# Attention masks moved from TensorE to VectorE in two chunks, and one score product a head instead of two in seven

## The chip, the cores and the metric

One Trainium2 chip, one of its cores. The metric is the device time of one execution in microseconds; the kernel before takes 721.85 us (median of three runs, 721.52 to 722.61).

## The reference

Three parts follow each other: windowed attention, a dense layer pair with an ELU between, and a layer of eight experts in which a token belongs to one expert by a greedy assignment with a capacity. Only the attention is touched here:

```python
# q, k, v: (4, 8, 576, 64), float32; window = 64, scale = 1/8
scores = scale * np.matmul(q, k.transpose(0, 1, 3, 2))
rel = pos[:, None] - pos[None, :]
mask = (rel >= 0) & (rel < window)          # a query sees itself and the 63 before it
scores = np.where(mask, scores, -1000000000.0)
scores = scores - np.max(scores, axis=-1, keepdims=True)
attn = np.exp(scores)
attn = attn / (np.sum(attn, axis=-1, keepdims=True) + 1e-09)
out = np.matmul(attn, v)
# x: (2304, 512) = out, heads side by side; h = x @ w_in; g = elu(h); y = g @ w_out
# logits = y @ w_gate; assignment of 2304 tokens to 8 experts of 288; relu(y @ w1[e]) @ w2[e]
```

## The kernel before

The 2304 tokens are 18 chunks of 128 (c = 0 to 17). A sequence has 576 tokens, four and a half chunks, so a sequence begins at chunk 0, in the middle of chunk 4, at chunk 9 and in the middle of chunk 13. A chunk is two blocks of 64 queries. A block of queries needs 128 keys: its own 64 and the 64 ahead of them. For block 1 both halves lie in the chunk; for block 0 the half ahead is the second half of the chunk before.

A chunk goes through steps that are written as functions:

- `att_s1` transposes queries and keys on TensorE (four 128x128 transposes each, into the PSUM tiles "tp") and copies them to SBUF on ScalarE as `QT` and `KT`. `KT[c]` holds the keys as [rows of two heads, half of the chunk, pair of heads, 64 keys].
- `att_s2` makes the scores: the PSUM tiles `SC[0]` and `SC[1]`, one for a block, [128, 4, 128]. On the partitions stand the 64 queries of one of two heads, along them four pairs of heads and 128 keys. With `on_pe` true a mask product (line 301) writes the mask into the whole tile first, 0 or -2^40, from an identity and a bf16 mask tile, and the score products add to it. With `on_pe` false the score products write alone. Each product has 64 rows and 64 columns of weights (the queries of one head in one block). Block 1 takes one product a head over 128 keys (line 312, both halves of the chunk). Block 0 takes two: the own 64 keys (line 316) and, unless a sequence begins there, the 64 ahead from `KT[c - 1]` (line 319). The operands are float32, and each product is two passes, thus two rows in the trace. Eight heads in two blocks are 16 products of 64 columns on line 316 and 319 together and 8 of 128 on line 312: 48 passes.
- `att_exp` takes the row maxima on VectorE (line 336) and the exponentials on ScalarE (line 338). Where the mask isn't in the scores yet, VectorE adds it first, from PSUM to the SBUF tile `P` (line 333), and maximum and exponential read `P`. Now that is so from chunk 10 on.
- `att_norm` divides by the sums on VectorE (line 351); `att_s3` transposes `P` on TensorE (line 359) and copies it on ScalarE (line 361); `att_s4` multiplies it with the values (line 369) and hands the rows to the first layer (lines 386, 387). Block 1's values are the chunk's own, `V[c]`; block 0's are a tile `VP[c]` with the own 64 in its first half of partitions and the 64 ahead in the second, filled by two DMAs from SP.

In `attention` the order of one round is: `att_s1(c)`, the two `att_s3(c - 1)`, `att_s2(c)`, `att_exp(c)`, `att_norm(c)`, `att_s4(c - 1)`. From chunk 4 on the rounds are woven with the dense layers: `weave` takes from several streams in proportion to given weights, and so writes the program's order. Around this change the order is: the first layer of tile 2 with chunk 7; the second layer of tile 0 with chunks 8 to 10 and the rest of the preparation of w_out (`prep_wout`: three bit operations, a ScalarE and a VectorE step for each of 16 pieces, the last of which stands behind `att_s3(8, 1)`); the second layer of tile 1 with the next three rounds; that of tile 2 with three more, with the gate's weights (`prep_g2`) and some logits; the first layer of tile 3 with what is left of attention. A scheduler then orders each engine's instructions with a clock of its own: an instruction that is not ready by that clock lets later ones of the program pass. Each engine runs its queue in order, so an instruction whose operands are late holds up those behind it.

The PSUM banks are "mm" (three, the layers' products), "tp" (two, transposes and small products), "sc" (two, the scores) and "pv" (one). `a2` is a pool of SBUF tiles that is opened before the second layer of tile 1, when the rounds have reached chunk 10.

Of the kernel before, what the change touches and what calls it, by code (L numbers as in the profile page):

```python
# [7 lines left out]
F32 = mybir.dt.float32  # L8
# [37 lines left out]
def attention_moe_moe2_kernel(ctx: ExitStack, tc: tile.TileContext, q, k, v, w_in, w_out, w_gate, w1, w2, out):  # L46
    nc = tc.nc
# [11 lines left out]
    ND = DM // 128  # L59
# [17 lines left out]
    def bank(tag, bufs, shape=(128, 512), dt=F32):  # L77
        return ps.tile(list(shape), dt, name="ps_" + tag, tag=tag, bufs=bufs)
# [30 lines left out]
    masks = consts.tile([128, 2, 2, 128], BF)  # L109
# [125 lines left out]
            last["rows"] = ins.ins  # L235


    QN, KN, QT, KT, V, VP, P, PT, XT = ({} for _ in range(9))

    def rows(src, n, m):  # L240
        b, s = divmod(n, S)
        return src[b, :, s:s + m, :].rearrange("h s d -> s h d")

    def load(src, c, name, bufs=3):
        t = att.tile([128, H, D], F32, name=name, bufs=bufs)
        n = 128 * c
        while n < 128 * (c + 1):
            m = min(128 * (c + 1) - n, S - n % S)
            p0 = n - 128 * c
            nc.sync.dma_start(t[p0:p0 + m], rows(src, n, m))  # L250
            n += m
        return t
# [6 lines left out]
    def load_v(c):  # L259
        if c < NCH:  # L260
            V[c] = load(v, c, "vn")
            if c:
                VP[c] = att.tile([128, H, D], F32, name="vp", bufs=3)
                nc.sync.dma_start(VP[c][:64], rows(v, 128 * c, 64))
                nc.sync.dma_start(VP[c][64:], rows(v, 128 * c - 64, 64))

    def att_s1(c):
        KT[c] = att.tile([128, 2, ND, 64], F32, name="kt", bufs=3)
        pq = bank("tp", 2, [128, ND, 128])
        for i in range(ND):  # L270
            with tc.issue_after(last["qt", c]) if c in (2, 3, 4) else ExitStack():
                nc.tensor.transpose(pq[:, i], QN[c][:, 2 * i:2 * i + 2, :].rearrange("p h d -> p (h d)"), ident)  # L272
        QT[c] = att.tile([128, ND, 128], F32, name="qt", bufs=2)
        if c == 1:
            nc.vector.tensor_scalar(QT[c], pq, 0.125, None, op0=OP.mult)
        else:
            nc.scalar.activation(QT[c], pq, AF.Copy, scale=0.125)
        pk = bank("tp", 2, [128, 2, ND, 64])
        for i in range(ND):
            t = nc.tensor.transpose(pk[:, :, i], KN[c][:, 2 * i:2 * i + 2, :].rearrange("p h d -> p (h d)"), ident)  # L280
        if c == 0:
            last["kt"] = t.ins
        if c == 1:
            nc.vector.tensor_copy(KT[c], pk)
        else:
            nc.scalar.activation(KT[c], pk, AF.Copy)

    SC = {}

    def att_s2(c):
        for blk in range(2):
            SC[blk] = bank(*(("mm", 3) if c == 1 else ("sc", 2)), [128, ND, 128])
        half = [slice(0, 64), slice(64, 128)]
        first = [int((128 * c + 64 * blk) % S == 0) for blk in range(2)]
        on_pe = c < 10 or bool(first[0])
        for blk in range(2 if on_pe else 0):
            with tc.issue_after(last["kt"]) if c < 2 and c + blk else ExitStack():  # L300
                nc.tensor.matmul(SC[blk], identb, masks[:, blk, first[blk], None, :].to_broadcast([128, ND, 128]),
                                 start=True, stop=False)
        for i in range(ND):
            for n in range(2):
                for blk in range(2):
                    for h in range(2):
                        if blk == 1 and n == 1:
                            continue
                        r, o = half[h], half[h ^ blk]
                        w = QT[c][r, i, 64 * blk:64 * blk + 64]  # L310
                        if blk == 1:
                            t = nc.tensor.matmul(SC[1][o, i], w, KT[c][r, :, i], start=not on_pe, stop=not on_pe or i == ND - 1)  # L312
                            if c < 3:
                                last["sc"] = last["qt", c + 1] = t.ins
                        elif n == 0:
                            nc.tensor.matmul(SC[0][o, i, :64], w, KT[c][r, 0, i], start=not on_pe,  # L316
                                             stop=not on_pe or i == ND - 1 and bool(first[0]))
                        elif not first[0]:
                            nc.tensor.matmul(SC[0][o, i, 64:], w, KT[c - 1][r, 1, i], start=not on_pe,
                                             stop=not on_pe or i == ND - 1)  # L320

# [2 lines left out]
    def att_exp(c):  # L324
        mx = att.tile([128, 2, ND], F32, name="mx")
        rs = RS[c] = att.tile([128, 2, ND], F32, name="rs")
        for blk in range(2):
            first = [int((128 * c + 64 * b) % S == 0) for b in range(2)]
            P[c, blk] = att.tile([128, ND, 128], F32, name="sm", bufs=4)
            sc = SC[blk]  # L330
            if c >= 10 and not first[0]:
                sc = P[c, blk]
                nc.vector.tensor_tensor(sc, SC[blk], masks[:, blk, first[blk], None, :].to_broadcast([128, ND, 128]),
                                        op=OP.add)
            with tc.issue_after(last["max"]) if c == 1 and blk else ExitStack():
                last["max"] = nc.vector.tensor_reduce(mx[:, blk], sc, axis=AX.X, op=OP.max, negate=True).ins  # L336
            for i in range(ND):
                nc.scalar.activation(P[c, blk][:, i], sc[:, i], AF.Exp, bias=mx[:, blk, i:i + 1],
                                     accum_out=rs[:, blk, i:i + 1])
# [55 lines left out]
    def attention(a, b):  # L395
        for c in range(a, b + 1):
            if c < b:
                att_s1(c)
                load_qk(c + 3)
                yield 1500  # L400
            if c > a:
                att_s3(c - 1, 0)
                yield 500
                att_s3(c - 1, 1)
                yield 500
            if c < b:
                att_s2(c)
                att_exp(c)
                att_norm(c)
            if c > a:  # L410
                att_s4(c - 1)
                load_v(c + 2)
            yield 1500

    def early():
        def scores(c):
            att_s2(c)
            att_exp(c)
            att_norm(c)

        for part in (lambda: att_s1(2), lambda: load_qk(5), lambda: scores(2), lambda: att_s1(3), lambda: load_qk(6),
                     lambda: scores(3), lambda: att_s3(2, 0), lambda: att_s3(2, 1), lambda: att_s4(2), lambda: load_v(5),
                     lambda: att_s3(3, 0), lambda: att_s3(3, 1), lambda: att_s4(3), lambda: load_v(6)):
            with tc.high_priority():
                part()
            yield 1

    a2 = []
    a2_ctx = ExitStack()

    NF32 = 1
# [636 lines left out]
    for c in range(2):  # L1068
        att_s1(c)
        load_qk(c + 3)  # L1070
    for c in range(2):
        att_s2(c)
        att_exp(c)
# [114 lines left out]
```

## Time and profile before

| | |
|---|---|
| median of three runs | 721.85 us (721.52 to 722.61) |
| profiled execution | 725.0 us, its span 723.3 us |
| granted TensorE clock, mean | 0.998 |
| TensorE busy | 702.1 us, 97% |
| VectorE busy | 434.9 us, 60% |
| ScalarE busy | 354.7 us, 49% |
| GpSimd busy | 166.7 us, 23% |
| chain that ended last | TensorE 72%, issue 14%, VectorE 6%, ScalarE 4% |

Busy shares are means over stages; products are pipelined and their records overlap, so what one costs in a run of equal ones is the distance from start to start. In the rows PE is TensorE's products, PEld its weight loads, DVE VectorE, ACT ScalarE, POOL GpSimd; L312 is line 312. A time is in microseconds from the start of the span.

### The profile page before, as it was taken

What the parts mean: (1) busy time and instruction counts of PE and PEld (TensorE: products, weight loads), DVE (VectorE), ACT (ScalarE), POOL (GpSimd) and SP (SyncE); (2) the same over time, 40 slices, a digit from 0 to 9 for tenths busy, and PEclk for the clock granted to TensorE, in tenths of its full rate; (3) what the DMA queues carried; (4) which work ended last, traced back from release to release, by engine and by line L of the source; (5) the groups of instructions that cost most, each with busy time, mean ns of one, the idle gap of its engine ahead of it and who ended that gap; (6) DMA issues with size and microseconds to landing.
All of it is one profiled execution on the core that took longest, in us unless ns stands there. A gap on an engine that the chain in (4) does not pass through costs nothing.

```text
span 723.3 us, 15666 instructions
## 1 busy us (share of the span) xinstructions
PE 702.1 (97%) x6350; PEld 431.5 (60%) x6350; DVE 434.9 (60%) x1027; ACT 354.7 (49%) x853; POOL 166.7 (23%) x267
## 2 busy tenths in 40 slices
PE   7889999999999999999999999999989999999996
PEld 4768778656655555554545544444766566566662
DVE  4888998964343766455544556665556556465630
ACT  4369988776454646444454231010155554564630
POOL 2000000020100354444441343544232210210001
PEclk9999999999999999999999999999999999999999
DMA  9997564597466721001010220220179787677401
GB/s 232 365 246 153 137 149 132 143 169 160 105 123 128 110 51 61 1 1 59 1 58 18 74 86 18 88 74 30 59 193 337 236 262 253 237 232 232 144 30 44
DMA packets 137881, 94.56 MB, mean 131 GB/s; under 512 B 116496, under 2 KB 116752, under 8 KB 137808
## 3 DMA queue, kind: packets, MB, share of 16 engines
q1 hardware_dynamic: 134848, 83.85, 43.3%
q0 software_dynamic: 2960, 9.70, 4.1%
q8 instruction: 50, 0.82, 0.5%
q14 instruction: 23, 0.19, 0.1%
HBM read 73.94 MB, written 9.70 MB: 116 GB/s over the span
## 4 chain that ended last, share of the span: by engine, by line
PE 72%; issue 14%; DVE 6%; ACT 4%; POOL 2%; DMA 1%; SPq 0%; POOLq 0%; ACTq 0%; DVEq 0%
PE ps_mm L555 25%; PE ps_mm L477 20%; PE ps_mm L1022 6%; PE ps_pv L369 3%; PE ps_tp L1006 2%; PE ps_sc L1006 2%; PE ps_mm L461 2%; PE ps_tp L359 2%; POOL out_dram L990 1%; PE ps_sc L749 1%; DVE mx L336 1%; PE ps_sc L312 1%; PE ps_sc L316 1%; PE ps_tp L272 1%; PE ps_tp L280 1%
## 5 line engine op out<-in xcount | busy, mean ns | idle before, releaser
L555 PE MATMUL ps_mm<-slab,g 128*128 128x512 f16 (+1 forms) x912 | 202.1, 367 | 0.0
L477 PE MATMUL ps_mm<-xt,slab 128*128 128x512 f16 (+1 forms) x960 | 174.6, 336 | 1.5 <-DVE xt L387 0.8
L477 PEld LDWEIGHTS <-slab 128*128 128x128 f16 x960 | 91.2, 98 | 69.0 <-issue 2.5
L555 PEld LDWEIGHTS <-g 128*128 128x128 f16 x912 | 79.8, 98 | 69.6
L1022 PE MATMUL ps_mm<-xet,slab 128*128 128x288 f16 (+2 forms) x768 | 98.1, 280 | 2.7 <-issue 2.2
L923 DVE SCALAR_TENSOR_TENSOR slab<-raw,slab 128x512 f16<-128x512 f32 x112 | 73.6, 687 | 39.0 <-ACT slab L922 33.7
L1022 PEld LDWEIGHTS <-slab 128*128 128x128 f16 x840 | 76.9, 98 | 28.9 <-issue 5.9
L480 ACT ACTIVATE r<-ps_mm 128x512 f32<-128x512 f32 x64 | 38.3, 599 | 65.7 <-PE ps_mm L477 52.0
L1006 PEld LDWEIGHTS <-h 128*32 128x32 f16 (+2 forms) x768 | 43.6, 99 | 44.7 <-issue 4.2
L922 ACT ACTIVATE slab<-raw 128x512 f16<-128x512 f32 x112 | 65.6, 624 | 0.3 <-DMA raw<-in_moe_w_dram 0.3
L489 DVE TENSOR_TENSOR r<-ps_mm,r 128x512 f32<-128x512 f32 x64 | 44.0, 688 | 29.7 <-POOL r L488 28.1
L591 ACT ACTIVATE r<-ps_mm 128x512 f32<-128x512 f32 x17 | 10.1, 595 | 100.8 <-PE ps_mm L555 90.0
L494 DVE TENSOR_TENSOR g<-r,g 128x512 f16<-128x512 f32 x64 | 44.3, 693 | 24.3 <-POOL g L493 22.9
L1006 PE MATMUL ps_sc<-slab,h 128*32 128x512 f16 (+2 forms) x384 | 53.2, 380 | 0.6 <-issue 0.3
L1006 PE MATMUL ps_tp<-slab,h 128*32 128x512 f16 (+2 forms) x384 | 52.6, 379 | 0.0
L1029 DVE SCALAR_TENSOR_TENSOR h<-ps_mm,h 128x288 f16<-128x288 f32 x61 | 27.7, 455 | 35.6 <-ACT h L1028 35.4
L1028 ACT ACTIVATE h<-ps_mm 128x288 f16<-128x288 f32 x61 | 25.0, 410 | 42.0 <-PE ps_mm L1022 41.4
L488 POOL TENSOR_SCALAR r<-r 128x512 f32<-128x512 f32 x48 | 33.6, 699 | 48.5 <-ACT r L481 48.2
L481 ACT ACTIVATE r<-r 128x512 f32<-128x512 f32 x64 | 40.5, 633 | 1.5
L990 POOL DMA_INDIRECT out_dram<-orow,idx x18 | 17.6, 979 | 93.5 <-ACT orow L1012 91.2
L493 POOL TENSOR_SCALAR g<-r 128x512 f16<-128x512 f32 x48 | 30.1, 627 | 38.4 <-DVE r L489 33.8
L537 POOL TENSOR_TENSOR xs<-r,xs 128x512 f16<-128x512 f32 x17 | 20.0, 1178 | 81.6 <-ACT xs L592 50.1
(235 smaller groups left out, 1016.4 us busy)
## 6 DMA issues: line engine op xcount, KB each, us to landing
raw<-in_moe_w_dram SPq DMA_DIRECT2D x32, 1024.0 KB, 5.4
slab<-in_moe_w_in_dram SPq DMA_DIRECT2D x16, 512.0 KB, 8.1
st<-in_moe_w_out_dram SPq DMA_DIRECT2D x16, 512.0 KB, 6.3
x2d<-xs SPq DMA_DIRECT2D x18, 256.0 KB, 2.8
vp<-in_v_dram SPq DMA_DIRECT2D x34, 128.0 KB, 4.4
qn<-in_q_dram SPq DMA_DIRECT2D x16, 256.0 KB, 5.1
kn<-in_k_dram SPq DMA_DIRECT2D x16, 256.0 KB, 4.9
vn<-in_v_dram SPq DMA_DIRECT2D x16, 256.0 KB, 4.9
```

The lines of the kernel that those rows point to most:

```text
L477: nc.tensor.matmul(ph[:, i], wi[d, (f + i) // 8][:, a, (f + i) % 8 * 128:((f + i) % 8 + 1) * 128], XT[t][:, b, d, :n], start=m == 0, stop= ...
L480: nc.scalar.activation(r, ph, AF.Relu, scale=-1.0 / A_H)
L481: last["act"] = nc.scalar.activation(r, r, AF.Exp, scale=-1.0).ins
L488: nc.gpsimd.tensor_scalar(r, r, -1.0, A_H, op0=OP.add, op1=OP.mult)
L489: nc.vector.tensor_tensor(r, ph, r, op=OP.max)
L493: last["pool"] = nc.gpsimd.tensor_scalar(hi, r, 1.0, 1.0, op0=OP.mult, op1=OP.mult).ins
L494: nc.vector.tensor_tensor(lo, r, hi, op=OP.subtract)
L555: pe(nc.tensor.matmul(px, g[:, f % fg, a, 128 * i:128 * i + 128], wo[f // 2][:, b, f % 2, cols], start=f + m == 0, stop=f == NF - 1 and m ...
L922: dv(nc.scalar.activation(t[:, 0, c], st[:, g], AF.Copy, scale=64.0))
L923: dv(nc.vector.scalar_tensor_tensor(t[:, 1, c], st[:, g], 64.0, t[:, 0, c], op0=OP.mult, op1=OP.subtract))
L1006: t = nc.tensor.matmul(po[p0 + k:p0 + k + step], H2[e][:, a, f, s0 + k:s0 + k + step], W2[e][f // 2][:, b, f % 2, :], start=m == 0, stop=m ...
L1022: last["e1"] = nc.tensor.matmul(ph[:, r], W1[e][d][:, a, f * 128:(f + 1) * 128], XET[e][:, b, d, r], start=m == 0 and r.start == 0, stop=m ...
```

## The change

From chunk 8 on, instead of chunk 10, the mask is added by VectorE, in chunk 9 for block 0 too, which makes the products with the keys ahead there although a sequence begins (the mask rules all of them out). From chunk 11 on a new tile `K2[c]` in the pool `a2` holds the second half of the chunk before and then the first half of the chunk, copied by VectorE from `KT[c - 1]` in SBUF and from the PSUM tile of the key transposes; block 0 takes one product a head over it, 128 columns. The order of keys in block 0 is then ahead, own; so the mask is block 1's, and the two halves of `VP` change places.

```diff
@@ load_v
             if c:
                 VP[c] = att.tile([128, H, D], F32, name="vp", bufs=3)
-                nc.sync.dma_start(VP[c][:64], rows(v, 128 * c, 64))
-                nc.sync.dma_start(VP[c][64:], rows(v, 128 * c - 64, 64))
+                own, ahead = (slice(64, 128), slice(0, 64)) if c >= JOINED else (slice(0, 64), slice(64, 128))
+                nc.sync.dma_start(VP[c][own], rows(v, 128 * c, 64))
+                nc.sync.dma_start(VP[c][ahead], rows(v, 128 * c - 64, 64))
@@ att_s1  (JOINED = 11)
         else:
             nc.scalar.activation(KT[c], pk, AF.Copy)
+        if c >= JOINED:
+            K2[c] = a2[0].tile([128, 2, ND, 64], F32, name="k2", bufs=2)
+            nc.vector.tensor_copy(K2[c][:, 0], KT[c - 1][:, 1])
+            nc.vector.tensor_copy(K2[c][:, 1], pk[:, 0])
@@ att_s2
-        on_pe = c < 10 or bool(first[0])
+        on_pe = c < 8
...
+                        elif c in K2:
+                            if n == 0:
+                                nc.tensor.matmul(SC[0][o, i], w, K2[c][r, :, i], start=True, stop=True)
                         elif n == 0:
                             nc.tensor.matmul(SC[0][o, i, :64], w, KT[c][r, 0, i], start=not on_pe,
                                              stop=not on_pe or i == ND - 1 and bool(first[0]))
-                        elif not first[0]:
+                        elif not first[0] or not on_pe:
                             nc.tensor.matmul(SC[0][o, i, 64:], w, KT[c - 1][r, 1, i], start=not on_pe,
                                              stop=not on_pe or i == ND - 1)
@@ att_exp
-            if c >= 10 and not first[0]:
+            if c >= 8:
                 sc = P[c, blk]
-                nc.vector.tensor_tensor(sc, SC[blk], masks[:, blk, first[blk], None, :].to_broadcast([128, ND, 128]),
+                nc.vector.tensor_tensor(sc, SC[blk], masks[:, blk or int(c in K2), first[blk], None, :].to_broadcast([128, ND, 128]),
                                         op=OP.add)
```

## Rows read from the trace of the kernel before

**Rows 1.** Busy time by stretches: stretch, length, PE, PEld, DVE, ACT, POOL (instructions), clock, DMA, GB/s.

```profile
120.00:140.00 20.00, 20.00 (x269) 15.09 (x268) 18.82 (x36) 16.04 (x41) 0.00 (x0) 1.00 0.56 158
140.00:160.00 20.00, 20.00 (x173) 11.58 (x169) 16.01 (x31) 12.91 (x46) 3.45 (x22) 1.00 0.78 162
...
240.00:260.00 20.00, 20.00 (x214) 11.27 (x212) 15.53 (x40) 11.37 (x31) 8.09 (x12) 1.00 0.50 80
```

**Rows 2.** Who waited for whom, 120 to 300 us: total, times, longest.

```profile
ACT r L480 <- PE ps_mm L477: 20.9, 17, 2.1
...
DVE sm L333 <- PE ps_sc L319: 17.2, 6, 5.2
```

**Rows 3.** Chain that ended last: start, duration; a pair of mask products.

```profile
133.09 0.43 PE ps_sc L301 x2
```

**Rows 4.** TensorE in order of time, chunk 8's scores: start, duration, engine, line, operation, shapes.

```profile
138.21 0.27 PE L316 MATMUL ps_sc<-kt,qt 64*64 64x64 f32 x2
...
139.28 0.34 PE L369 MATMUL ps_pv<-pt,vp 128*64 128x64 f32 x4
```

**Rows 5.** TensorE in order of time, chunk 9's scores.

```profile
150.42 0.27 PE L316 MATMUL ps_sc<-kt,qt 64*64 64x64 f32 x2
...
150.53 0.28 PE L316 MATMUL ps_sc<-kt,qt 64*64 64x64 f32 x4
...
150.82 0.28 PE L316 MATMUL ps_sc<-kt,qt 64*64 64x64 f32 x4
150.92 0.60 PE L312 MATMUL ps_sc<-kt,qt 64*64 64x128 f32 x8
151.46 0.34 PE L369 MATMUL ps_pv<-pt,vp 128*64 128x64 f32 x4
```

**Rows 6.** TensorE in order of time, chunk 11's scores in two parts.

```profile
171.61 0.27 PE L316 MATMUL ps_sc<-kt,qt 64*64 64x64 f32 x2
...
172.11 1.09 PE L359 MATMUL ps_tp<-ident,sm 128*128 128x128 f32 x8
173.13 0.33 PE L312 MATMUL ps_sc<-kt,qt 64*64 64x128 f32 x2
...
173.93 0.28 PE L369 MATMUL ps_pv<-pt,vp 128*64 128x64 f32 x2
```

**Rows 7.** TensorE in order of time, chunk 17's scores in two parts.

```profile
275.01 0.27 PE L316 MATMUL ps_sc<-kt,qt 64*64 64x64 f32 x2
...
275.62 0.66 PE L359 MATMUL ps_tp<-ident,sm 128*128 128x128 f32 x4
276.21 0.27 PE L316 MATMUL ps_sc<-kt,qt 64*64 64x64 f32 x2
...
276.82 0.39 PE L369 MATMUL ps_pv<-pt,vp 128*64 128x64 f32 x6
```

**Rows 8.** VectorE's groups by form, 0 to 300 us: count, busy us, mean ns, idle before.

```profile
L333 DVE TENSOR_TENSOR sm<-ps_sc,masks 128x512 f32<-128x512 f32 x16 | 10.3, 684 | 17.2 <-PE ps_sc L319 17.2
...
L484 DVE TENSOR_SCALAR r<-r 128x512 f32<-128x512 f32 x8 | 3.3, 417 | 0.8 <-ACT r L481 0.8
...
L284 DVE COPY kt<-ps_tp 128x512 f32<-128x512 f32 x1 | 0.7, 678 | 0.0
```

**Rows 9.** VectorE in order of time.

```profile
147.24 1.29 DVE L351 TENSOR_TENSOR sm<-sm,rs 128x512 f32<-128x512 f32 x2
...
152.70 0.69 DVE L133 SCALAR_TENSOR_TENSOR slab<-b,slab 128x512 f16<-128x512 f32 x1 [0.70 <-ACT slab L132]
...
205.21 0.17 DVE L225 TENSOR_SCALAR G<-gsum 128x8 f16<-128x8 f32 x1
...
227.20 1.09 DVE L225 TENSOR_SCALAR G<-gsum 128x8 f16<-128x8 f32 x2
```

**Rows 10.** TensorE in order of time, second layer of tile 0 and chunk 11's key transposes.

```profile
153.47 7.29 PE L555 MATMUL ps_mm<-slab,g 128*128 128x512 f16 x33
...
164.61 0.60 PE L280 MATMUL ps_tp<-ident,kn 128*128 128x128 f32 x4
```

More of the change, by code (lines that the diff above doesn't have):

```diff
@@ L235, in pe @@
             last["rows"] = ins.ins
-    QN, KN, QT, KT, V, VP, P, PT, XT = ({} for _ in range(9))
+    QN, KN, QT, KT, K2, V, VP, P, PT, XT = ({} for _ in range(10))
+    JOINED = 11
+    a2 = []
     def rows(src, n, m):
@@ L426, in early @@
             yield 1
-    a2 = []
     a2_ctx = ExitStack()
```

## The prediction

> **What bounds the kernel now.** I read the busy time by stretches first [rows 1]: from 120 us, where the chunks of this change begin, TensorE is busy 20.00 of 20 us at a granted clock of 1.00, while VectorE is busy 18.82 of 20 from 120 us, 16.01 from 140 and 15.53 from 240. Next the list of waits from 120 to 300 us [rows 2]: the others wait for TensorE. VectorE stood 17.2 us in front of six mask additions (longest 5.2) because the scores were not there yet, and ScalarE waited 17 times, 20.9 us in all, for a finished first-layer product. The reader is to see that in this stretch the time is TensorE's own stream, and that VectorE has to be late by more than its slack before it costs anything. So I price the change in TensorE time and treat VectorE work as a risk. Behind this stretch the same instructions follow in the same order; a saving there should arrive at the end whole. The profiled execution is 725.0 us, 723.3 of span and 1.7 around it, 3.15 above the median of the three runs; the sum is made on it and the difference carried over to the median.
>
> **Masks of chunks 8 and 9.** Each chunk loses two mask products. A pair takes 0.43 us of TensorE [rows 3], and the two chunks hold two such pairs: -0.86 us. They stand among products of the same full-array kind, so no change of array shape goes with them. Chunk 9 begins a sequence, so today it leaves out the eight products with the keys ahead; afterwards it makes them, masked to nothing. Its scores take 150.42 to 151.46, 1.04 us [rows 5]; chunk 8, which already makes them, 138.21 to 139.28, 1.07 us [rows 4]: +0.03 us.
>
> **The joined product, seven chunks (11 to 17).** What it saves depends on what the score products wait for. In chunk 9 [rows 5] the 64-column passes of block 0 follow each other, two at a time for the two halves of the rows, at (150.82 - 150.53)/5 = 0.058 us; the 128-column passes of block 1 (eight in 0.60 us, four pairs, the last of 0.27) at (0.60 - 0.27)/3 = 0.11 us. Both go on at once: block 1's last pass starts some 0.8 us after its first, no later than eight pitches of its own ask. Four quarters of the array thus run side by side, and a stretch of scores lasts as long as its longer stream plus a tail: chunk 9, 8 x 0.11 = 0.88, tail 0.16. Chunk 8 has 16 passes of 0.058 = 0.93 in block 0 against 0.88 in block 1; with a tail of 0.15 that is the 1.07 measured. Joining two passes of 64 into one of 128 saves 2 x 0.058 - 0.11, some 0.01 us: the columns are the same. Block 0 becomes 8 x 0.11 = 0.88, as long as block 1.
>
> The larger part comes from balance. From chunk 10 on the score products are cut in two by the transposes of the chunk before. Chunk 11 has 0.50 (171.61 to 172.11) and 0.80 us (173.13 to 173.93), 1.30 in all [rows 6]: in the first part block 0 was the longer (6 x 0.058), in the second block 1 (6 x 0.11), and both excesses are paid. With equal streams a cut chunk costs 0.88 + 2 x 0.15 = 1.17, so 0.13 less. Chunk 17, whose cut falls in the middle, has 0.61 + 0.61 = 1.22 [rows 7] and saves 0.05. These are the first and the last of seven; I take their mean, 0.09, times 7: -0.63 us. Bounds: a cut that parts block 0's first pair from block 1's (0.22 us alone, then 0.88 and two tails: 1.40 against 1.30) loses 0.10 each, +0.7; no cut at all (1.04 against 1.30) gains 0.26 each, -1.8. I stay near what rows 6 and 7 show since nothing in the change moves the cut far.
>
> The Trainium skill says otherwise on what is hidden: the page TensorE: Matmul & The Clock Gate, Part 3, The mechanism, has a weight load overlap running products only where the row group differs. Blocks 0 and 1 share row groups, so by that rule each load would stand in line and a joined product would save eight loads a row group and chunk. The streams in rows 5 speak against it. It is a rival below.
>
> **Where the cut falls in chunks 8 to 10.** Masks on VectorE read the scores once more. One takes 0.684 us [rows 8], two in a row about 1.2: chunk 8's probabilities, ready now at 147.24 + 1.29 = 148.53 [rows 9], come 1.2 us later and chunk 9's scores, at 150.42, may then be the ones that are cut. A cut costs 1.30 - 1.07 = 0.23 us in products and some 0.1 in transposes: 0 to +0.3. The other way, chunk 10's cut may fall behind its scores: -0.3 to 0. I take 0.
>
> **VectorE's additions.** Four mask additions: 4 x 0.684 = 2.7 us, 2.4 when they follow each other. They land where VectorE splits the last quarter of the second weights. The last split ends at 152.70 + 0.69 = 153.39 [rows 9]; of the 33 second-layer products from 153.47 [rows 10] the split's six are the 26th to 31st, so they start near 153.47 + 25 x 0.215 = 158.8 (0.215 is a mask product's share of its pair, as wide as these). The slack is 5.4 us, 2.4 goes: free. If it were gone, all of it would show. Exponentials then read SBUF in place of PSUM, on ScalarE, which waits for TensorE anyway.
>
> Two copies a joined chunk. From PSUM, 256 columns: a 512-column copy took 0.678 us [rows 8], an 8-column operation 0.17 [rows 9]; between them I take 0.42. Within SBUF: a 512-column operation took 0.417 [rows 8], so between 0.17 and 0.42, I take 0.29. Together 0.7, seven times: 5 us of VectorE, in no chain that ends last. The scores of chunk 11 wait for them, but its key transposes start at 164.61 [rows 10] and the scores at 171.61 [rows 6], 7 us for a delay of about 1; the PSUM bank of the keys is held by as much and next wanted by the transposes at 172.11. Queued behind the copies on VectorE are the mask additions, normalisation and, in the fourth tile's first layer, the chain that frees the product banks. The values ahead change halves of the tile: the same two transfers, of the same size, in the same place of SP's queue.
>
> One row shows a price that can be higher: an 8-element operation took 0.17 us at 205.21 and two took 1.09 at 227.20 [rows 9], a stretch in which GpSimd works (0.00 us from 120, 8.09 of 20 from 240 [rows 1]). The Trainium skill has a rule for it (SBUF — State Buffer, Who interferes with whom): a copy within SBUF on VectorE may need a port pair that GpSimd holds for a whole instruction. With 0.4 us more for each of the last three chunks' copies the sum stays, as nothing waits for VectorE there by less than a microsecond on average.
>
> **Sum.** -0.86 + 0.03 - 0.63 = -1.46 us: the profiled execution from 725.0 to 723.5, the median from 721.85 to 720.4. Cut points included, 718.9 to 722.0 for this case alone.
>
> **Rivals.**
> 1. *The streams pay for their loads* (the rule above). For: the joined form drops eight loads a row group and chunk. Against: 24 products of two passes, 24 loads a row group, fit in 1.07 us with all the streaming. Were loads the limit, a load would cost 1.07/24 = 0.045 us, eight of them 0.36, seven chunks 2.5: with the masks -3.3, 718.5.
> 2. *The saving is given back in cuts.* The scheduler sets the cut from its own clock; if it parts the blocks unequally in the joined chunks (+0.7) and cuts chunk 9 (+0.3): -0.86 + 0.03 + 0.7 + 0.3, 722.0: no change. For: every chunk from 10 on is cut today. Against: its products now come in equal pairs.
> 3. *VectorE becomes late* (slower). In the fourth tile's first layer (15.53 of 20 us busy in its middle [rows 1]) a copy that heads VectorE's queue before its transposes are done holds up the work that frees product banks. The slack is 20.9/17 = 1.2 us on average [rows 2]; from there on TensorE stands. If a copy waits as long as the longest wait in front of a mask addition, 5.2, TensorE loses 4.0: 720.4 + 4.0 = 724.4. Against: in that stage the mask additions hardly waited; the transposes precede the copies by little.
> 4. *The joining changes nothing*, as the columns are equal: only the masks count, -0.83, 721.0.
> 5. *No chunk is cut any more*: 1.04 against 1.30, -1.8 instead of -0.63: 719.2. For: the probabilities of chunks 8 and 9 move by more than a stretch of scores lasts. Against: nothing new in the later chunks lies between scores and probabilities.
>
> **How the numbers follow.** A measurement here tells 0.2%, 1.44 us, from no change, so my sum stands on that line. Forecast 0.48, split evenly by it; rival 1 0.06; rival 2 0.14; rival 3 0.10; rival 4 0.08; rival 5 0.10; the rest, 0.04, is an order further on that turns out worse. Faster 0.24 + 0.06 + 0.10 = 0.40; same 0.24 + 0.14 + 0.08 = 0.46; slower 0.10 + 0.04 = 0.14. The range, 718.8 to 723.2, leaves out rival 1 and most of rival 3.
>
> **What would show it.** Chunks 8 and 9 without mask products, 0.86 us less on that line; block 0's joined passes at the pitch 0.11, block 1's unchanged; a cut chunk's scores near 1.17 and an uncut one near 1.04; TensorE still 20 of 20 from 120 to 300. Wrong: a pitch of joined passes below 0.11 (rival 1), parts whose sum is above 1.30 (rival 2), TensorE waiting for a bank or for a copy between 225 and 300 (rival 3).

## The result: slower, 728.41 us against 721.85

The changed kernel takes 728.41 us (median of seven, 728.0 to 734.53); the kernel before, on the same chip, 721.85 (seven, 721.52 to 724.27). The recorded ratio is 1.0118, interval 1.010 to 1.0136 (it comes with its interval and is not the quotient of the two medians, which is 1.0091; the same holds for the table below). By the medians that is 6.6 us more where 1.5 less was forecast, and outside the range. The profiled execution of after is 728.01 us (span 726.3).

To see where the time came, equal products of the two traces are set against each other. The 381st first-layer product starts at 129.24 us in before, ahead of everything that the change touches; the 301st second-layer product at 377.48, behind it. In after the first is 0.10 later, the second 8.04. I call the difference, 7.94 us, the shift across the stretch, and give it for every kernel below. It is larger than the difference of the two executions (3.0) because before's profiled execution lost some 5 us more than after's behind 520 us (TensorE busy 17.03 of 20 us from 520 to 540 us, 19.30 in after); the medians differ by 6.6. On the chain that ended last VectorE has 10% (before 6%), TensorE 66% (72%). A time in which TensorE waits is called a stand.

Busy time of after by stretches (columns as in [rows 1]):

```profile
120.00:140.00 20.00, 20.00 (x266) 15.06 (x265) 18.82 (x37) 16.16 (x42) 0.00 (x0) 1.00 0.57 158
140.00:160.00 20.00, 18.06 (x171) 10.15 (x166) 15.61 (x31) 11.89 (x43) 3.45 (x22) 0.91 0.67 134
240.00:260.00 20.00, 20.00 (x199) 11.41 (x198) 15.28 (x38) 11.99 (x32) 8.32 (x12) 1.00 0.64 108
300.00:320.00 20.00, 18.86 (x242) 11.34 (x241) 11.15 (x23) 7.74 (x14) 8.87 (x12) 0.91 0.01 2
```

The last of these stretches in before:

```profile
300.00:320.00 20.00, 20.00 (x183) 10.42 (x182) 9.46 (x17) 8.13 (x14) 8.13 (x13) 1.00 0.00 1
```

In two of the four stretches TensorE is no longer busy all the time, and in the same two its clock is 0.91. What it waited for, 140 to 318 us in after (total, times, longest; before has no such row at all in this stretch):

```profile
PE ps_tp L369 <- DVE sm L361: 1.9, 1, 1.9
PE ps_tp L222 <- DMA wt<-slab: 1.2, 1, 1.2
PE ps_mm L486 <- DVE r L498: 0.6, 2, 0.3
PE ps_tp L513 <- DVE logits L516: 0.4, 1, 0.4
PE ps_tp L533 <- ACT pt L371: 0.2, 1, 0.2
```

**The stand at 152.** Chunk 9's scores in after, TensorE in order of time:

```profile
149.21 0.27 PE L326 MATMUL ps_sc<-kt,qt 64*64 64x64 f32 x2
...
149.82 0.27 PE L319 MATMUL ps_sc<-kt,qt 64*64 64x128 f32 x1
152.03 0.63 PE L369 MATMUL ps_tp<-ident,sm 128*128 128x128 f32 x4 [1.94 <-DVE sm L361]
...
152.95 0.66 PE L369 MATMUL ps_tp<-ident,sm 128*128 128x128 f32 x4
...
154.09 3.58 PE L564 MATMUL ps_mm<-slab,g 128*128 128x512 f16 x9
```

In [rows 5] chunk 9's scores ran through; here chunk 8's transposes stand in their middle and wait. From the last score product to the first transpose 2.21 us pass, 2.10 more than usual. Behind it the layer products go at 3.58/9 = 0.40 us each, in place of 0.215. That is the lower clock level (two stretches of after, at 153.7 and at 310.7):

```profile
153.70:157.10 3.40, 3.40 (x20) 1.34 (x17) 2.86 (x5) 1.40 (x4) 0.79 (x6) 0.50 0.00 0
310.70:314.10 3.40, 3.07 (x13) 1.22 (x13) 2.20 (x4) 1.04 (x3) 2.56 (x4) 0.50 0.02 5
```

TensorE works 3.40 and 3.07 us there at 1.2 GHz in place of 2.4, so it loses half of that, 1.7 and 1.5 us. What made chunk 8's probabilities late is in VectorE's order of time:

```profile
142.54 1.28 DVE L343 TENSOR_TENSOR sm<-ps_sc,masks 128x512 f32<-128x512 f32 x2
143.74 0.68 DVE L133 SCALAR_TENSOR_TENSOR slab<-b,slab 128x512 f16<-128x512 f32 x1
144.34 1.27 DVE L346 TENSOR_REDUCE mx<-sm 128x4 f32<-128x512 f32 x2
...
149.80 0.17 DVE L354 TENSOR_SCALAR rs<-rs 128x8 f32<-128x8 f32 x1
149.92 0.69 DVE L128 SCALAR_TENSOR_TENSOR b<-st,b 128x512 uint32<-128x512 uint32 x1
150.53 0.20 DVE L355 RECIPROCAL rs<-rs 128x8 f32<-128x8 f32 x1
150.64 0.64 DVE L133 SCALAR_TENSOR_TENSOR slab<-b,slab 128x512 f16<-128x512 f32 x1
151.20 1.29 DVE L361 TENSOR_TENSOR sm<-sm,rs 128x512 f32<-128x512 f32 x2
```

They are ready at 152.49, against 148.53 in [rows 9]: 3.96 us later. The masks themselves are 1.28 of it. The rest is others' work that now falls between the links of the chain: a split between masks and maxima, the evacuation of the next queries and keys on ScalarE between the exponentials, a bit operation and a split between sum, reciprocal and normalisation.

**The stand at 305.** Behind chunk 17's last value products after has no layer products left to run. Groups of TensorE, 303 to 316 us:

```profile
L486 PE MATMUL ps_mm<-xt,slab 128*128 128x512 f16 x20 | 6.0, 459 | 0.3 <-DVE r L498 0.3
L513 PE MATMUL ps_tp<-G,g 128*128 128x16 f16 x72 | 4.2, 169 | 0.6 <-DVE logits L516 0.4
L514 PE MATMUL ps_tp<-G,g 128*128 128x8 f16 x70 | 4.0, 166 | 0.0
```

The small gate products of tile 3 (L513, L514; tiles are counted from 0 here, so this is the prediction's fourth, and what the expectations call the third) come in one run of 140 (128 of tile 3's, then 12 of tile 4's); in before they come in runs of 32 with 24 layer products between (counted in its trace). The run has stands of 0.55, 0.21, 0.25 and 0.44 us, 0.41 stands ahead of it, and a lower clock level lies behind. Why no layer product was there is a row of GpSimd, 290 to 318 us. In after, and then in before (a row not shown so far):

```profile
POOL g L502 <- PE ps_pv L379: 12.5, 1, 12.5
```

```profile
POOL g L493 <- PE ps_pv L369: 1.1, 1, 1.1
```

The first layer of tile 4 writes its `g` into memory that attention frees with its last value product. Until then its products can run ahead only as far as three tiles `r` and three PSUM banks "mm" hold their results: six groups of twelve products, which with the 576 of the tiles before make 648. The traces stop there too (counted): after has used all 648 before the last value product (at 306.2), before 608 (at 292.3), so before has 16 more at once and then runs of 24.

The stands add up to 2.10 + 1.40 (at 222.9, start to start, for the gate's transposed weights, which a transposing DMA of `prep_g2` fetches) + 0.52 (at 269.5) + 1.86 (at 305) = 5.9 us, the two clock stretches to 3.2: 9.1. Less the savings below (0.9), 8.2; the shift is 7.9.

### The profile page after: what moved, and what is told of

Same layout as the page of the kernel before. It is cut to its first block, busy times and chain, and to the rows that moved or that the text cites. A ratio compares the mean times of both kernels' runs of the same rounds, so it can differ in the third digit from the quotient of the medians.

```text
span 726.3 us, 15482 instructions
## 1 busy us (share of the span) xinstructions
PE 703.5 (97%) x6250; PEld 430.4 (59%) x6250; DVE 440.9 (61%) x1045; ACT 355.4 (49%) x853; POOL 171.5 (24%) x267
## 4 chain that ended last, share of the span: by engine, by line
PE 66%; issue 14%; DVE 10%; ACT 4%; DMA 3%; POOL 2%; SPq 0%; POOLq 0%; DVEq 0%; ACTq 0%
PE ps_mm L564 23%; PE ps_mm L486 18%; PE ps_mm L1031 6%; PE ps_mm L470 3%; PE ps_tp L1015 2%; PE ps_sc L1015 2%; PE ps_pv L379 2%; PE ps_tp L369 2%; POOL out_dram L999 1%; DMA kn<-in_k_dram 1%; DVE mx L346 1%; DVE g L503 1%; PE ps_sc L758 1%; DVE r L498 1%; DVE b L128 1%
## 5 line engine op out<-in xcount | busy, mean ns | idle before, releaser
L564 PE MATMUL ps_mm<-slab,g 128*128 128x512 f16 (+1 forms) x912 | 203.5, 369 | 0.0
L564 PEld LDWEIGHTS <-g 128*128 128x128 f16 x912 | 80.1, 98 | 71.0 <-issue 2.4
L497 POOL TENSOR_SCALAR r<-r 128x512 f32<-128x512 f32 x48 | 35.4, 737 | 41.9 <-ACT r L490 41.2
```

What stands on the lines that cost most here:

```text
L497: nc.gpsimd.tensor_scalar(r, r, -1.0, A_H, op0=OP.add, op1=OP.mult)
L564: pe(nc.tensor.matmul(px, g[:, f % fg, a, 128 * i:128 * i + 128], wo[f // 2][:, b, f % 2, cols], start=f + m == 0, stop=f == NF - 1 and m ...
```

## The experiments

Each kernel was timed beside the kernel before on the same chip; "before" is the median there. Three of the four chips run the kernel before some 7 us slower than the fourth; in their traces 346 to 350 us pass from the 301st second-layer product to the end, on the fourth 341 (345 in join_nocopy). The shift across the stretch leaves that part out. A diff is against the changed kernel, those of copies_only and burst_gate against the kernel before.

| kernel | us | before | ratio [interval] | shift, us |
|---|---|---|---|---|
| masks_only | 729.42 | 727.66 | 1.0009 [0.9985, 1.0033] | +2.81 |
| join_only | 731.87 | 727.66 | 1.0050 [1.0026, 1.0074] | +4.35 |
| maskless8 | 728.88 | 727.66 | 1.0007 [0.9981, 1.0032] | +1.55 |
| chunk8_back | 730.20 | 727.66 | 1.0025 [1.0003, 1.0048] | +3.85 |
| copies_only | 721.52 | 720.67 | 1.0008 [0.9995, 1.0021] | +1.84 |
| join_nocopy | 723.46 | 720.67 | 1.0034 [1.0022, 1.0047] | +2.75 |
| burst_gate | 722.07 | 720.67 | 1.0014 [0.9996, 1.0031] | +1.95 |
| after_again | 728.71 | 720.67 | 1.0119 [1.0090, 1.0148] | +6.09 |
| late_chunk8 | 727.00 | 728.39 | 0.9984 [0.9963, 1.0005] | -0.54 |
| chunk9_masks | 727.20 | 728.39 | 0.9980 [0.9959, 1.0002] | -0.31 |
| masks_again | 730.70 | 728.39 | 1.0040 [1.0021, 1.0060] | +1.60 |
| join_again | 730.98 | 728.39 | 1.0035 [1.0014, 1.0056] | +3.95 |
| mended | 731.50 | 728.21 | 1.0059 [1.0037, 1.0081] | +5.10 |
| late_chunk8_again | 727.36 | 728.21 | 0.9988 [0.9974, 1.0001] | -0.53 |
| chunk9_masks_again | 726.97 | 728.21 | 0.9986 [0.9969, 1.0003] | -0.28 |
| after_third | 733.87 | 728.21 | 1.0095 [1.0070, 1.0121] | +8.93 |

### The two halves of the change, and the stand at 152

**masks_only**: the masks' part alone.

```diff
-    JOINED = 11
+    JOINED = 99
```

> The masks of chunks 8 and 9 on VectorE, no joined products. Theory A (the masks of chunk 8 make its probabilities late where VectorE is full; TensorE's queue stands 2.1 us in front of their transposes at 152 us, and its clock is at the lower level for some 3.4 us behind it, 1.7 us lost): the same stall and the same stretch of lower clock at about 152 us, nothing of the later waits at 223 and 305 us; 3.8 - 0.8 = 3.0 us above before, about 724.9. Theory B (the joining alone does it): no stall, 0.8 below before, 721.0.

**join_only**: the join alone.

```diff
-        on_pe = c < 8
+        on_pe = c < 10
-            if c >= 8:
+            if c >= 10:          # att_exp
```

> The joined products of chunks 11 to 17, masks as before. Theory A+ (two faults: the later waits, 1.4 us for the gate's transposed weights at 223 us and 1.9 us in the gate products at 305 to 311 us with another stretch of lower clock behind them, come with the joined products): no stall at 152 us, these later waits there, some 4 to 5 us less what the joined products save (0.6 to 0.9): 725 to 726. Theory A alone (the later waits are only what the late chunk 8 left behind): 721.2.

The stand at 152 comes with the masks (2.10 us, and the lower clock level behind it), the run of gate products and, in these two traces, the wait of 1.5 us for the transposed weights with the join. The shifts add up to 7.16 of after's 7.94; after's stand of 0.52 us at 269.5, which neither half has, is most of the rest.

**maskless8**: masks_only, and chunk 8 gets no mask at all (`if c >= 9` in att_exp).

> masks_only, but chunk 8 gets no mask at all, neither by TensorE nor by VectorE; the computation is changed by that. It takes away VectorE's two additions and leaves TensorE's part as in masks_only. Theory A: no stall at 152 us, no lower clock there, 0.8 below before: 721.0. Rival (TensorE stands because the scheduler puts the transposes earlier once the mask products are gone, whatever VectorE does): the stall stays, about 724.9.

**chunk8_back**: the whole change, but chunk 8 keeps its mask products (`on_pe = c < 9`, `if c >= 9`).

> The changed kernel with chunk 8's masks back on TensorE (chunk 9's stay on VectorE, products joined from 11 on). Theory A: without the stall, below the changed kernel by 3.8 less 0.43: about 725.0. If all of the loss hangs on chunk 8: about 721. Rival (VectorE is too late in any chunk): chunk 9's transposes stand instead, still 728.

In neither does TensorE stand at 152 (busy 20.00 of 20 us from 140 to 160 in both), so it is VectorE's work for chunk 8's mask that brings the stand. At 160 us maskless8 has gained 0.81 us, the two mask pairs' price nearly to the digit. Its shift is positive all the same, by two waits for the transposed weights, in an order that has no join. Waits of TensorE in maskless8, 140 to 318 us:

```profile
PE ps_tp L222 <- DMA wt<-slab: 1.4, 2, 0.8
```

So that wait is not the join's alone: burst_gate and masks_again, without a join, have it at 0.2, copies_only at 0.6, and before's one trace has none. chunk8_back's shift, 3.85, is the join's less the one mask pair.

**masks_again** and **join_again** repeat the halves on another chip. Waits of TensorE, 140 to 318 us, first in masks_again, then in join_again:

```profile
PE ps_tp L369 <- DVE sm L361: 1.9, 1, 1.9
PE ps_tp L222 <- DMA wt<-slab: 0.2, 1, 0.2
```

```profile
PE ps_tp L222 <- DMA wt<-slab: 1.2, 1, 1.2
PE ps_tp L513 <- DVE logits L516: 0.4, 1, 0.4
PE ps_mm L486 <- DVE r L498: 0.3, 1, 0.3
```

> The mask part alone, measured again beside the join alone, on the chip of this call, for the sum. Theory: the stall of 2.1 us near 152 with or without a lower clock level behind it (1.7 us), less 0.8 saved: +1.3 to +3.0 us, 0.2 to 0.4% above before. Rival (the earlier 1.0009 holds): within 0.15% of before.

> The join alone, measured again beside the masks alone, on the chip of this call. Theory: no stall near 152; a run of some 140 gate products near 305 with 1 to 1.9 us of waits and a lower clock level behind it (1.7 us), a wait of up to 1.5 us for the transposed weights near 217: +3 to +5 us at 375 us, 0.4 to 0.7% above before, and with the masks alone 0.8 to 1.1%, the whole change's. Rival (masks and join do not add up): the two sum to 0.6% or less.

masks_again has the same stand and no lower clock level behind it; compare the clock, 1.00, with after's 0.91 at the same busy time, 18.06 (140 to 160 us):

```profile
140.00:160.00 20.00, 18.06 (x168) 10.21 (x164) 15.72 (x32) 12.40 (x44) 3.45 (x22) 1.00 0.64 135
```

Its shift, 1.60, is smaller than that of masks_only by 1.2. The clock thus falls behind this stand in some executions (after, after_third, masks_only) and not in others (masks_again, after_again). By the ratios the halves sum to 0.6% on the first chip (0.8% by the medians) and 0.75% on this one, where the whole change took 0.95 to 1.19% on other chips; by shift 5.55 of after_again's 6.09. The scatter of the times leaves open whether anything is missing there.

**late_chunk8**: masks_only with chunk 8's transposes given out later; VectorE's work is the same.

```diff
@@ attention, before "if c > a"
+            if c == 9:
+                att_s2(c)
+                att_exp(c)
+                att_norm(c)
+                yield 4000
+                for blk in range(2):
+                    att_s3(c - 1, blk)
+                    if blk == 0:
+                        yield 250
+                att_s4(c - 1)
...
@@ att_s3
-        with tc.issue_after(last["stir"]) if c == 0 else ExitStack():
+        behind = last["stir"] if c == 0 else last["l2"].ins if c == 8 else None
+        with tc.issue_after(behind) if behind is not None else ExitStack():
```

> The mask part alone (as in the run of the masks alone: VectorE masks from chunk 8 on, no join), with one edit: chunk 8's transposes are given out behind chunk 9's scores and nine further second-layer products, instead of in the middle of the scores. VectorE's work is the same. Theory (the 2.1 us stall near 152 is a matter of place: the order puts the transposes 3 us ahead of the probabilities): no wait above 0.3 us between 140 and 165, no lower clock level there, layer products 0.5 to 1 us ahead of before at 165, time 0.0 to 0.2% below before. Rival (VectorE's longer chain holds up TensorE wherever the transposes stand): a wait of 1 us or more remains, +1 to +3.5 us at 165.

> Masks on VectorE from chunk 8, its transposes placed late, no join; measured again, for a narrower interval. Theory (0.8 us saved, no stall): 0.9985 to 1.0000 of before, 0.5 to 0.8 ahead at 375 us of where it stood before chunk 8. Rival (the earlier 0.9984 was that chip's scatter): 1.000 to 1.002.

(`last["l2"]` is the newest second-layer product.) The stand is gone. Chunk 8's probabilities are as late as in masks_again (normalised from 150.88 on, there from 150.87), but in late_chunk8_again the transposes come at 151.93, behind nine layer products, and wait for nothing; TensorE in order of time, then 140 to 160 us:

```profile
149.97 2.12 PE L578 MATMUL ps_mm<-slab,g 128*128 128x512 f16 x9
151.93 0.60 PE L370 MATMUL ps_tp<-ident,sm 128*128 128x128 f32 x4
```

```profile
140.00:160.00 20.00, 20.00 (x180) 11.26 (x177) 16.79 (x32) 12.11 (x43) 0.00 (x0) 1.00 0.44 106
```

The stand was a matter of place. The clock stays at 1.00. The shift is -0.54 and -0.53; of the 0.8 saved, 0.2 went into a wait for the transposed weights. Both ratios lie below 1 and both intervals hold it.

**chunk9_masks**: masks on VectorE from chunk 9 (`on_pe = c < 9`, `if c >= 9`, JOINED = 99).

> The mask part one chunk later and no join: VectorE masks from chunk 9 on, chunk 8 keeps its two mask products. Theory: chunk 8's probabilities are as early as before, so no stall near 152; one mask pair less (0.43) against chunk 9's eight extra products: 0.3 to 0.45 us ahead of before at 165 and at 375 us, apart from waits for the transposed weights that differ between executions; gate products in runs of 32 as before; time within 0.1% of before. Rival (any mask moved to VectorE here costs a stall): +2 us or more.

> Masks on VectorE from chunk 9, no join; measured again, for a narrower interval. Theory (0.3 to 0.4 us saved): 0.9990 to 1.0000 of before. Rival: 1.000 to 1.002.

As forecast, -0.31 and -0.28. With late_chunk8 it is the best version found, some 0.1 to 0.2% below before, no further than a measurement tells from no change.

### What the join costs

**copies_only**: before, with the two copies into a tile that nothing reads.

```diff
+            k2 = a2[0].tile([128, 2, ND, 64], F32, name="k2", bufs=2)
+            nc.vector.tensor_copy(k2[:, 0], KT[c - 1][:, 1])
+            nc.vector.tensor_copy(k2[:, 1], pk[:, 0])
```

> The kernel before with the change's two VectorE copies for chunks 11 to 17 (nothing reads the second tile) and its product form and masks unchanged. Theory (the join's price is the order of TensorE's stream, which the shorter score products shift; the copies are not in it): the order stays that of before, layer products shifted by 0 +- 0.6 us at 375 us, no wait for the transposed weights near 217, gate products in runs of 32 between layer products, time within 0.3% of before. Rival A (VectorE's copies delay what frees banks): +2 to +4 us at 375 us, as in the join alone (+4.30). Rival B (half and half): +1 to +2.

**join_nocopy**: join_only with the chunk's own keys in place of the copies.

```diff
-            K2[c] = a2[0].tile([128, 2, ND, 64], F32, name="k2", bufs=2)
-            nc.vector.tensor_copy(K2[c][:, 0], KT[c - 1][:, 1])
-            nc.vector.tensor_copy(K2[c][:, 1], pk[:, 0])
+            K2[c] = KT[c]
```

> The join alone, but the joined products read the chunk's own key tile and the two copies are not made (the half ahead is thus taken from the chunk's own second half: part of the computation is changed). Masks as before. Theory (order): the order is that of the join alone, so the wait near 217 us (about 1.5), the run of 140 gate products near 304 with its waits (about 1.5) and a lower clock level of some 3.4 us behind it return: +3.5 to +4.5 us at 375 us, as in the join alone (+4.30), time 0.4 to 0.7% above before. Rival A (copies): 0 +- 0.6 at 375 us, time like before.

By time the theory about holds (1.0008, and 1.0034 where at least 1.004 was expected). join_nocopy, which by its edit takes wrong keys for the half ahead, has the run of 140 gate products and the lower clock level behind it (306.9 to 310.3) without any copy, copies_only has neither. GpSimd's wait for the last value product, 290 to 318 us, first in join_nocopy, then in copies_only:

```profile
POOL g L500 <- PE ps_pv L377: 6.5, 1, 6.5
```

```profile
POOL g L502 <- PE ps_pv L379: 1.1, 1, 1.1
```

The first has used 648 first-layer products at that point, the second 620. But the copies are not free: copies_only is shifted by 1.84, where the theory said 0.6 at most. 0.6 of it is the wait for the transposed weights. Another 0.7 is in the scores: those of chunks 11 to 17 take 9.75 us in its trace and 9.07 in before, because chunks 14 and 16 are cut into more parts; so the copies move the order a little too. The other half microsecond was not located. And join_nocopy, at 2.75, is 1.2 to 1.6 below the join with its copies and has no wait for these weights. Without that wait, 1.46 and 1.32 us, the join's two traces would be shifted by 2.9 and 2.6, as join_nocopy is. So what the copies add to the join's price is at most this wait; whether they cause it is open, since maskless8 has it without them.

**burst_gate**: before, with tile 3's gate products given out together.

```diff
-    weave((chain(take(l4, 4), spread(gate(3), l4, 2), l4, take(l5, 4), spread(gate(4), l5, 2), l5), UT * 4))
+    weave((chain(take(l4, 4), gate(3), l4, take(l5, 4), spread(gate(4), l5, 2), l5), UT * 4))
```

> The kernel before with one edit far from masks and keys: the third tile's gate products are given out together instead of spread between the fourth tile's first-layer products; TensorE's order becomes 64, 2 layer products, 64 in place of four runs of 32 with 24 layer products between. Theory (a run of gate products outpaces what it waits for, and the clock falls behind it): nothing changes up to 300 us; between 300 and 375 us +2.5 to +4 us, of them 1 to 2 in waits and 1.5 to 1.8 at the lower clock level, and the difference stays to the end: about 0.4% slower. Rival (the run of gate products costs nothing by itself; the join's price there has another cause): 0 +- 0.5 us at 375 us, same time.

Runs of 64, 2 layer products, 64: the clock falls behind them, with no wait of TensorE there; from 300.9 us:

```profile
300.90:304.30 3.40, 3.40 (x10) 1.24 (x9) 0.58 (x2) 0.00 (x0) 0.00 (x0) 0.50 0.00 0
```

So a run of gate products was followed by the lower level without any stand, in the one trace taken, 1.7 us; the waits that I expected with it stayed out. By time burst_gate can't be told from before. The waits are the join's, and the counts above point to the missing layer products.

**after_again**, **after_third**, and **mended**: the whole change with late_chunk8's order, and with each gate sum of tile 3 held behind tile 4's first-layer products given out so far (`last["l1"]` is the newest).

```diff
@@ gate
+                with tc.issue_after(last["l1"]) if t == 3 and f == 0 else ExitStack():
+                    pe(nc.tensor.matmul(pl, g[:, f % fg, 0, 128 * i:128 * i + 128], G2[:, f, :], start=f == 0, stop=False))
```

> The changed kernel on the same chip as the other kernels of this call. Theory (masks and join add up): at 375 us its layer products stand 7.1 +- 1 us behind before (2.79 of the masks alone and 4.30 of the join alone), time 0.8 to 1.1% above before. Rival (on a chip where the masks alone read 1.0009 the whole change reads like the join alone): ratio 1.004 to 1.006.

> The changed kernel once more, beside the mended one on the same chip. Theory: 6 to 8 us behind before at 375 us (the larger figure where the clock falls behind the stall at 152), time 0.8 to 1.2% above before and 0.7 to 1.1% above the mended one. Rival (its distance to the mended kernel is under 3 us): then the two places are not its cause.

> The whole change (masks on VectorE from chunk 8, joined products and copies from chunk 11), with two edits of order alone: chunk 8's transposes behind nine further second-layer products, and each of the third tile's four gate sums behind the fourth tile's first-layer products given out so far, so that the gate products run as 64, 32, 32 with 24 layer products between. Theory (the price is the order): no stall near 152; no wait for the gate sums and no or one lower clock level near 305; a wait of up to 1.4 us for the transposed weights near 217 may stay: at 375 us -0.5 to +2 us against before (the changed kernel: 6 to 8), time 0.7 to 1.1% below the changed kernel. Rival A (the copies and joined products cost by themselves): +3 us or more at 375 us. Rival B (the 64 gate products in a row bring the lower clock level as in the run with the gate products given out together): +1.7 on top of theory's.

Half of the expectation for mended failed. The stand at 152 is gone, as in late_chunk8, and so is the wait for the weights. At 304.8 a single longer stand took the place of the run of 140 (waits of TensorE, 140 to 318 us; then the lower clock level):

```profile
PE ps_mm L500 <- DVE r L512: 3.2, 1, 3.2
```

```profile
303.50:310.30 6.80, 5.53 (x14) 1.94 (x14) 4.17 (x7) 1.90 (x5) 4.59 (x6) 0.50 0.00 0
```

3.4 us of stand, start to start, and 2.8 lost to the clock (half of the 5.53 us worked there). Against after's 7.94 the shift should lose the stand at 152 with its clock stretch (3.8), the weights' wait (1.40) and the stand at 269.5 (0.52), and gain 6.2 in place of 3.4 here: 5.0; it is 5.10. The gate products in one run were thus not the cause but what filled the hole: GpSimd waited 12.4 us for the last value product here too, and 648 first-layer products were used up. Holding them back laid the hole bare. mended takes 0.3% less than after (731.50 to 733.87), not the 0.7 to 1.1% expected; by these numbers alone that is the rivals' side (2.4 us, where one named under 3; a shift of 5.10, where another named 3 or more), and only the trace, with the new stand at 304.8, speaks against them. No run gives the join its layer products back at the end of attention, so that their lack is what costs there is argued from the counts: 648 and a stand in every trace with the join, 584 to 620 and no stand there in every trace without it. after's two traces here differ by their clock: after_third, with the lower level behind 152 and for 6.8 us behind 308.8, is shifted by 8.93, after_again, with one stretch of 3.4, by 6.09.

## Why the prediction was wrong

**What bounds the kernel.** Right as far as it went: TensorE's stream. Wrong was the sentence that the same instructions follow in the same order behind the stretch: both halves of the change moved the order of TensorE's stream.

**Masks, -0.86 + 0.03.** Right: maskless8 gained 0.81. A mask addition takes 0.683 us in after.

**The cut in chunks 8 to 10, "0 to +0.3, taken 0".** This step failed, and it failed first. I saw that chunk 9's scores might be the ones that are cut, and priced the cut as products and transposes that go on. I took chunk 8's probabilities to be 1.2 us later, the masks' own time, and did not ask when they are ready on the chip against where a cut would place their transposes. They were 3.96 later, because other work of VectorE and ScalarE fell between the links of the longer chain, and the cut put the transposes 2.1 us ahead of them: +2.1, and 1.7 more where the clock fell, for an edit that saves 0.8. VectorE's slack was reckoned only against the layer products of the last split (5.4 us, and that held), not against these transposes.

**The joined product, -0.63.** Mis-sized by a factor of eight. (In its working 0.88 + 2 x 0.15 is 1.18, not 1.17; nothing hangs on that.) The columns are the same, as said: chunk 12 in after, not cut, has 32 passes in 193.17 - 192.14 = 1.03 us, chunk 9 in [rows 5] 1.04. But the cuts part the two streams unequally:

```profile
177.79 0.33 PE L324 MATMUL ps_sc<-k,qt 64*64 64x128 f32 x2
...
178.38 1.09 PE L369 MATMUL ps_tp<-ident,sm 128*128 128x128 f32 x8
179.41 0.32 PE L319 MATMUL ps_sc<-kt,qt 64*64 64x128 f32 x1
...
180.21 0.39 PE L564 MATMUL ps_mm<-slab,g 128*128 128x512 f16 x1
...
192.14 0.33 PE L324 MATMUL ps_sc<-k,qt 64*64 64x128 f32 x2
...
193.17 0.63 PE L379 MATMUL ps_pv<-pt,vp 128*64 128x64 f32 x14
```

Chunk 11 takes 0.59 + 0.80 = 1.39 (1.30 in [rows 6]): the bound of 1.40 that I had named. Four of seven chunks are so; all seven take 9.00 us in join_only, 9.07 in before: -0.08.

**What the join moved.** Not in the sum at all. In chunks 11 and 13 eight layer products now pass ahead of the value products (eleven in join_nocopy; in after L564 follows chunk 11's scores at 180.21, in [rows 6] the value products do), and more in the chunks behind. Attention ends 40 layer products later in the stream, and they are missing when it ends. That the form of the products moves the order is shown by join_nocopy, which has no copies; how the scheduler comes to it was not looked at. "Nothing in the change moves the cut far" and "an order further on that turns out worse", to which I gave 0.04, are where this stood.

**VectorE's copies.** Sizes right (0.305 and 0.419 us, forecast 0.29 and 0.42); costing nothing is in doubt (copies_only). The 0.4 us more that the prediction allowed a late chunk's copies, for GpSimd working beside them, came out under 0.1: in after five of the copies within SBUF took 0.28 us, the two latest 0.35 and 0.37.

**Rivals.** Rival 1 fell: by it a joined chunk saves 0.36 us, and chunk 12 with 32 passes takes 1.03 where chunk 8 with 48 took 1.07 [rows 4]. The Trainium skill's rule behind it (TensorE: Matmul & The Clock Gate, Part 3, The mechanism) is not borne out by these rows. Rival 2 was right in its mechanism, cuts that part the blocks unequally, and missed the wait. Rival 3, the slower one, had the engine and the kind right, a late VectorE in front of transposes, but the place wrong (chunk 8, not the first layer of tile 3). Its own sign, TensorE waiting for a bank between 225 and 300, did appear, at 269.5 and worth 0.52 us where 4.0 was reckoned. Rival 4 was right on the score products alone (-0.08) and knew nothing of the order. Rival 5 came true in one of seven chunks in join_only (chunk 12).

**Open.** Why the wait for the transposed weights is 0 in some executions and 1.5 in others: the transfer took 4.4 to 4.7 us from issue to landing in before, 5.0 to 6.2 in after. Why the clock falls behind the stand at 152 in some executions only. And, as said under mended, whether the join would be free with layer products left for the end of attention.

## What to carry to other kernels

Where a scheduler orders the engines' queues, price a small edit twice: what it saves, and what its order puts in front of an operand that is now later; a saving of 0.8 us cost 2 to 4 by where one chunk's transposes stood, and moving them took that cost away. Delay of a chain is not the added instruction alone: count the work of the same engine that can slip in between its links (1.3 us added, 4.0 measured). And work that covers the end of a stage is a stock: an edit that lets it run earlier can show its price far away, where the stage ends (here argued from counts).

## What the runs showed of the hardware

128 narrow gate products (0.026 us apart) with two layer products in their middle and no wait were followed by 3.4 us at the lower clock level (burst_gate, one trace). So were the runs of 140, with stands of up to 0.55 us in them, in all seven traces that have one; runs of 32 with 24 layer products between were not, in eight traces. A stand of 2.1 us was followed by 3.4 us at that level in three traces and by none in two others of the same order of instructions there.
